# Two weight rows of the last column slab moved from the casting queue to five DMA engines of the hardware queue, cast on chip

## The chip, the cores and the metric

The kernel runs on one core of one Trainium2 chip. The metric is the device time of one execution in microseconds, as the median of several; the profile gives the span of one execution, about 1.8 us less. Before the change the time is 177.0 to 177.1 us.

## The reference, cut to what matters

Attention over 64 heads of 576 tokens (plain and dilated windows) gives `x`, 4608 tokens by 512. A soft mixture of experts follows; only its end matters here.

```python
logits = x @ phi                       # 32 slots, 4 per expert
slot_input = softmax_over_tokens(logits).T @ x
for e in range(8):
    h = np.maximum(slot_input[e] @ w1[e], 0.0)
    slot_out[e] = h @ w2[e]            # w2[e]: 1024 x 512, float32
out = softmax_over_slots(logits) @ slot_out    # 4608 x 512, float32
```

All eight `w1` and `w2` come from HBM as float32 and are used as bf16. The output is 9.44 MB of float32.

Of the kernel before, what the change touches and what calls it, by code (L numbers as in the profile page):

```python
# [7 lines left out]
ACTF = mybir.ActivationFunctionType  # L8
# [6 lines left out]
DM = H * D  # L15
# [43 lines left out]
class Sched:  # L59
# [8 lines left out]
    def op(self, eng, fn, dur, prio, reads=(), writes=(), rmw=(), after=(), banks=(), name="",  # L68
           kind="c", nbytes=0, rate=422e3, lag=0.0, sem=None, tail=False):
        o = Op()  # L70
        o.eng, o.fn, o.dur, o.prio, o.name = eng, fn, dur, prio, name
        o.kind, o.bytes, o.rate, o.lag, o.sem, o.tail = kind, nbytes, rate, lag, sem, tail
        o.deps, o.succ = set(), []
        o.banks, o.opens, o.ord = [], [], None
        o.seq = len(self.ops)
        for a in after:
            if a is not None:
                o.deps.add(a)
        for b in reads:
            o.deps.update(b.w)  # L80
            b.r.append(o)
        for b in writes:
            if b.r:
                b.prev = b.w + b.r
                b.w, b.r = [], []
            o.deps.update(b.prev)
            b.w.append(o)
        for b in rmw:
            o.deps.update(b.prev)
            o.deps.update(b.w)  # L90
            o.deps.update(b.r)
            b.w.append(o)
        for b in list(reads) + list(writes) + list(rmw) + list(banks):
            if isinstance(b, Bank) and b not in o.banks:
                o.banks.append(b)
                if b.left == 0:
                    o.opens.append(b)
                b.left += 1
        o.deps.discard(o)
        self.ops.append(o)  # L100
        return o
# [99 lines left out]
def bass_dilated_sliding_attn__then__soft_moe_slots_kernel(  # L201
# [15 lines left out]
    def take(n):  # L217
        o = top[0]
        top[0] = o + (n + 1) // 2 * 2
        return o  # L220
# [4 lines left out]
    o_kqv = [o_w2 + 3 * 8 * DM, take(3 * 2304)]  # L225
# [36 lines left out]
    def a(off, dims, p0=0, pn=128):  # L262
        return AP(ar, p0 * NBF + off, [[NBF, pn]] + dims)
# [4 lines left out]
    def af(off, dims, p0=0, pn=128):  # L268
        return AP(ar_f.tensor, (p0 * NBF + off) // 2, [[NBF // 2, pn]] + dims)
# [4 lines left out]
    def pf(bank, off, dims, p0=0, pn=128):  # L274
        return AP(ps, p0 * 4096 + bank * 512 + off, [[4096, pn]] + dims)
# [6 lines left out]
    op = sc.op  # L282
    PE, ACT, DVE, POOL, SP = "PE", "ACT", "DVE", "POOL", "SP"
    pe, act, dve, pool, spq = nc.tensor, nc.scalar, nc.vector, nc.gpsimd, nc.sync
# [4 lines left out]
    def actt(n, extra=0.0):  # L289
        return 0.2 + extra + n / 1200.0  # L290

    def dvet(n, psum=False):
        return ((120 if psum else 58) + n) / 960.0
# [3 lines left out]
    b_stg = [[[Buf(f"stg{i}{j}{x}") for x in range(2)] for j in range(3)] for i in range(NSTG)]  # L297
    b_kqv = [[[Buf(f"kqv{i}{j}{x}") for x in range(2)] for j in range(3)] for i in range(2)]
# [15 lines left out]
    b_w2h = [[Buf(f"w2h{x}{s}") for s in range(2)] for x in range(4)]  # L314
# [3 lines left out]
    def w2off(e):  # L318
        return o_w2 + e * 8 * DM if e < 5 else o_stg + (e - 5) * 8 * DM


    def sem(n):
        return [nc.alloc_semaphore(n), 0]

    s_stg = [[[sem(f"s_in{i}{j}{x}") for x in range(2)] for j in range(3)] for i in range(NSTG)]
    loads = {}
# [23 lines left out]
    wq = []  # L350
# [28 lines left out]
    def w2_slab(e, s, c0=0, n=8):  # L379
        def fn():  # L380
            return pool.dma_start(  # L381
                a(w2off(e) + 256 * s + c0 * DM, [[DM, n], [1, 256]]),
                moe_w2[e].rearrange("(p c) f -> p c f", c=8)[:, c0:c0 + n, 256 * s:256 * s + 256])
        return (fn, n << 17, f"w2s_{e}{s}{c0}", [b_w2[e][s] if e == 6 else b_w2h[(0, 4, 6, 7).index(c0)][s]])
# [1 line left out]
    wq += [w1_piece(e, 2 if e == 0 else 0) for e in range(8)]  # L386
    wq += [w2_piece(e) for e in range(6)] + [w2_piece(6, 0, 4)]
    for s in range(2):
        wq += [w2_slab(6, s, 4, 4), w2_slab(7, s, 0, 4), w2_slab(7, s, 4, 2),
               w2_slab(7, s, 6, 1), w2_slab(7, s, 7, 1)]  # L390
    nw = [0]

    def load_w(n):
# [17 lines left out]
       kind="dma", nbytes=1 << 20, sem=sem("s_w1f"), writes=b_w2[0], name="w1f")  # L411
# [401 lines left out]
    for x, y in zip(dma_order, dma_order[1:]):  # L813
# [4 lines left out]
    T1 = NH * PERIOD + 12.0  # L818
    op(DVE, lambda: dve.tensor_reduce(f(o_rcol, [[1, 1]]), f(o_csp, [[1, 16]]),
                                      mybir.AxisListType.X, AluOp.add), .2, T1, reads=[b_csp],  # L820
       writes=[b_rcol], name="cs")
# [4 lines left out]
    def sd_fn(bank=bank):  # L826
# [10 lines left out]
       reads=[bank], writes=[b_sit], name="sid")  # L837
    row_sums(5, 1, T1 + 4)
    for x in range(2):
# [12 lines left out]
        for g in range(2):  # L852
            op(PE, lambda g=g, l1_fn=l1_fn: l1_fn(g), pet(4, 760), T1 + 0.2 + x + .5 * g,
               reads=[b_sit] + b_w1[4 * g:4 * g + 4], rmw=[bank], name=f"L1{g}{x}")
# [3 lines left out]
            writes=[b_hsb[x], b_p[0], b_p[1]], name=f"RL{x}")  # L858
# [10 lines left out]
    for g in range(2):  # L869
# [3 lines left out]
           reads=[bank], writes=[b_htz], name=f"HE{g}")  # L873
# [5 lines left out]
    def l2(es, x, col, n, cs=range(8), bufs=None):  # L879
# [22 lines left out]
       name="SOx")  # L902
    op(DVE, lambda: dve.tensor_copy(af(o_sx, [[1, 512]], 64, 64), pf(sobank[0].idx, 0, [[1, 512]], 64, 64)),
       dvet(512, True), T1 + 10, reads=[sobank[0]], writes=[b_sx, b_p[2]], name="SOy")
    for x in (1, 2):
        l2((6,), x, 256 * x - 256, 256, range(4, 8), [b_w2[6][x - 1]])
        for y, cs in enumerate((range(4), range(4, 6), range(6, 7), range(7, 8))):
            l2((7,), x, 256 * x - 256, 256, cs, [b_w2h[y][x - 1]])
        op(DVE, lambda x=x: dve.tensor_tensor(  # L909
            a(o_so + 256 * x - 256, [[1, 256]], 64, 64), pf(sobank[x].idx, 0, [[1, 256]], 64, 64),  # L910
            af(o_sx + 512 * x - 512, [[1, 256]], 64, 64), AluOp.add), dvet(256, True),
           T1 + 10 + 20 * x, reads=[sobank[x], b_sx], writes=[b_so[x - 1]], name=f"SO{x - 1}")



    NA = 2.5
    b_og = [[[Buf(f"og{G}{j}{s}") for s in range(2)] for j in range(n)] for G, (_, n) in enumerate(GROUPS)]
    store_ops = []
    ne = [0]
# [2 lines left out]
    def ostg(G):  # L922
        return o_w1 + 8 * GROUPS[G][0]
# [6 lines left out]
    def out_tile(G, j, c0, cw, prio):  # L930
        bank = Bank(f"o{G}{j}{c0}")
        t0, n = GROUPS[G]
        rd = [b_so[s] for s in range(2) if c0 < 256 * (s + 1) and c0 + cw > 256 * s]
        op(PE, lambda: pe.matmul(pf(bank.idx, 0, [[1, cw]]), a(o_et + t0 + j, [[n, 128]]),  # L934
                                 a(o_so + c0, [[1, cw]]), start=True, stop=True),
           pet(1, cw), prio, reads=[b_et] + rd, writes=[bank], name=f"O{G}{j}{c0}")
        dst = af(ostg(G) + 2 * (512 * j + c0), [[1, cw]])
        src = lambda: pf(bank.idx, 0, [[1, cw]])
        wr = [b_og[G][j][s] for s in range(2) if c0 < 256 * (s + 1) and c0 + cw > 256 * s] + over(G)
        sca = f(rcol(G) + j, [[1, 1]])  # L940
        if ne[0] % 2 == 0:
            op(ACT, lambda: act.activation(dst, src(), ACTF.Copy, scale=sca), actt(cw, .1),  # L942
               prio + .1, reads=[bank, b_rinv], writes=wr, name=f"OE{G}{j}{c0}")
        else:
            op(DVE, lambda: dve.tensor_scalar(dst, src(), sca, None, op0=AluOp.mult),  # L945
               dvet(cw, True) + .08, prio + .1, reads=[bank, b_rinv], writes=wr, name=f"OE{G}{j}{c0}")
        ne[0] += 1

    def store(G, c0, cw, prio, j0, n):
        t0, nj = GROUPS[G]  # L950
        rd = [b_og[G][j][s] for j in range(j0, j0 + n) for s in range(2)
              if c0 < 256 * (s + 1) and c0 + cw > 256 * s]
        dst = out[t0:t0 + 128 * nj, c0:c0 + cw].rearrange("(p j) f -> p j f", j=nj)[:, j0:j0 + n, :]
        src = af(ostg(G) + 2 * (512 * j0 + c0), [[512, n], [1, cw]])
        store_ops.append(op(SP, lambda: spq.dma_start(dst, src), .1, prio, kind="dma",
                            nbytes=128 * n * cw * 4, rate=347e3 if cw < 512 else 420e3,
                            sem=sem(f"s_o{G}{c0}{j0}"), reads=rd, name=f"ST{G}{c0}{j0}"))

    T2 = T1 + 40
    halves = [(n // 2, n % 2 * 2) for n in range(int(2 * NA))]  # L960
    for G, x in halves:
        for j in (x, x + 1):
            out_tile(G, j, 0, 256, T1 + 20 + G + .25 * x)
        store(G, 0, 256, T1 + 20 + G + .25 * x + .2, x, 2)
    for G, x in halves:
        for j in (x, x + 1):
            out_tile(G, j, 256, 256, T2 + 10 + G + .25 * x)
        store(G, 256, 256, T2 + 10 + G + .25 * x + .2, x, 2)
    for G, js in [(2, (2, 3))] + [(G, range(8)) for G in range(3, 6)]:
        for j in js:  # L970
            out_tile(G, j, 0, 512, T2 + 10 + G + .1 * j)
            if j == js[-1] or G == 3 and j == 3:
                n = 4 if G == 3 else len(js)
                store(G, 0, 512, T2 + 10 + G + .1 * j + .05, j + 1 - n, n)
# [11 lines left out]
    for o in order:  # L986
        c = o.sem if o.kind == "dma" else ctr[o.eng]
# [4 lines left out]
        for d in o.deps:  # L992
            if d.eng == o.eng == PE:
                continue
            s, val = d.ev
# [60 lines left out]
```

## The kernel before: the parts that the change touches

GpSimd issues nearly all loads on the software queue, which casts on the way. The last 1.5 experts of `w2` come as two column slabs of 256 columns each (`s`), in ever smaller pieces, so that the first half of the output columns can be computed and stored while the second slab still loads.

```python
def w2_slab(e, s, c0=0, n=8):
    def fn():
        return pool.dma_start(
            a(w2off(e) + 256 * s + c0 * DM, [[DM, n], [1, 256]]),
            moe_w2[e].rearrange("(p c) f -> p c f", c=8)[:, c0:c0 + n, 256 * s:256 * s + 256])
    ...
for s in range(2):
    wq += [w2_slab(6, s, 4, 4), w2_slab(7, s, 0, 4), w2_slab(7, s, 4, 2),
           w2_slab(7, s, 6, 1), w2_slab(7, s, 7, 1)]
...
for x in (1, 2):                       # x = 1, 2: first and second column half
    l2((6,), x, 256 * x - 256, 256, range(4, 8), ...)
    for y, cs in enumerate((range(4), range(4, 6), range(6, 7), range(7, 8))):
        l2((7,), x, 256 * x - 256, 256, cs, [b_w2h[y][x - 1]])
    op(DVE, ... dve.tensor_tensor(..., AluOp.add) ...)   # L909: "the add" of each half
```

After each add come the output tiles of 128 tokens: one matmul, one scaling copy out of PSUM (ScalarE and VectorE in turn), and stores on SyncE's hardware queue. Ten tiles (2.5 groups of four) are made by halves: their left columns after the first add, their right ones after the second. The other 26 are made whole, after the second add. "Cover" below means the stores of left halves, which keep the DMA engines busy until the second add lets the others go.

The softmax here doesn't subtract the row's maximum and nothing guards it: scores larger than these inputs give would overflow.

## Time and profile before

| | before |
|---|---|
| time, median | 177.03 us (176.88 to 177.2) |
| span of the profiled execution | 175.2 us |
| last weight row landed | 151.54 us |
| second add (L909) begins | 151.90 us |
| first store of the second half issued, landed | 153.35, 155.31 to 155.66 us |
| last store landed | 174.75 us |

Three more lines of the page say how the tail is fed. The first two are the scaling copies of the output tiles (busy time, mean ns, idle before); the third is the half-tile stores (KB each, us from issue to landing).

```profile
L942 ACT ACTIVATE ar<-ps,fs 128x512 f32<-128x512 f32 (+1 forms) x23 | 11.4, 636 | 5.7 <-PE ps L934 5.7
L945 DVE TENSOR_SCALAR ar<-ps,fs 128x512 f32<-128x512 f32 (+1 forms) x23 | 12.7, 627 | 1.0 <-PE ps L934 1.0
out_dram<-ar SPq DMA_DIRECT2D x10, 256.0 KB, 3.1
```

The mean of 0.63 us mixes half and whole tiles; a whole one takes about 0.75 us on either engine. So the two make a 262 KB tile every 0.38 us, faster than the queue drains it at about 430 GB/s (0.61 us). So once the second add is done the tail is stores alone, and its end is set by when they can begin and how many bytes are left then.

### The profile page before, as it was taken

To read this page: it belongs to the slowest core of one execution; us is meant where nothing else is said; L and a number is where in the kernel's file an instruction comes from. 1 tells how busy PE (TensorE), PEld (TensorE's weight loads), DVE (VectorE), ACT (ScalarE), POOL (GpSimd) and SP (SyncE) were. 2 spreads that over 40 slices of the span, in tenths; PEclk is the share of its full clock that TensorE was granted. 3 is DMA by queue.
4 is the path that set the end of the run, shared out by engine and by line. 5 is a ranking of instruction groups with operands and counts; after the bars stand their busy time and mean duration, and the time that the engine had idled before them with its cause. 6 is when DMAs were issued, how large, how long until landed. Compare 5 with 4: busy or idle time off the path is not lost.

```text
span 175.2 us, 4785 instructions
## 1 busy us (share of the span) xinstructions
PE 127.4 (73%) x2102; PEld 86.0 (49%) x2102; DVE 120.7 (69%) x220; ACT 105.1 (60%) x165; POOL 44.5 (25%) x90
## 2 busy tenths in 40 slices
PE   0008667969998998998988997999776766898000
PEld 0005535746766866776756766776343323442000
DVE  6899497978998998998698798349430002699300
ACT  2404763797978969969868968965603001599000
POOL 7659502406234053027200014940000000000000
PEclk9999995699999999999999999999999999999655
DMA  6999999999999999999999999999999999999997
GB/s 191 228 210 217 211 214 208 219 210 213 216 211 214 217 213 207 218 211 217 213 209 216 217 213 221 215 219 211 209 223 215 210 192 189 270 343 418 449 423 299
DMA packets 14388, 41.26 MB, mean 236 GB/s; under 512 B 1696, under 2 KB 7328, under 8 KB 12064
## 3 DMA queue, kind: packets, MB, share of 16 engines
q0 software_dynamic: 10512, 30.41, 88.3%
q1 hardware_dynamic: 3856, 10.55, 15.7%
q8 instruction: 16, 0.26, 0.5%
q14 instruction: 4, 0.03, 0.0%
HBM read 61.93 MB, written 9.44 MB: 407 GB/s over the span
## 4 chain that ended last, share of the span: by engine, by line
DMA 33%; DVE 24%; PE 22%; ACT 7%; POOL 5%; issue 3%; POOLq 0%; DVEq 0%
DMA ar<-in_moe_w_dram 21%; DMA ar<-in_v_dram 12%; PE ps L529 6%; DVE ar L497 6%; DVE ar L945 6%; ACT ar L568 4%; POOL ar L381 3%; DVE ar L503 3%; PE ps L590 2%; PE ps L713 2%; PE ps L536 2%; DVE ar L634 2%; PE ps L623 2%; PE ps L546 2%; DVE ar L454 2%
## 5 line engine op out<-in xcount | busy, mean ns | idle before, releaser
L568 ACT ACTIVATE ar<-ps 128x1152 bf16<-128x1152 f32 (+1 forms) x32 | 37.9, 1186 | 21.5 <-PE ps L553 10.9
L529 PE MATMUL ps<-ar 128*128 128x320 bf16 (+1 forms) x128 | 23.2, 306 | 16.1 <-DVE ar L503 13.8
L497 DVE STREAM_TRANSPOSE ar<-ar 128x576 uint32<-128x576 uint32 x28 | 32.8, 1237 | 0.6 <-DMA ar<-in_v_dram 0.6
L634 DVE TENSOR_TENSOR ar<-ps,fs 96x768 bf16<-96x768 f32 (+1 forms) x32 | 26.3, 822 | 1.1
L596 ACT ACTIVATE ar<-ps 128x768 bf16<-128x768 bf16 x32 | 24.8, 809 | 3.6 <-PE ps L590 3.1
L529 PEld LDWEIGHTS ps<-ar 128*128 128x128 bf16 x128 | 10.8, 100 | 20.9 <-POOL ar L427 13.7
L623 PE MATMUL ps<-ar 128*128 128x65 bf16 x320 | 15.2, 195 | 3.4 <-ACT ar L568 2.1
L590 PE MATMUL ps<-ar 128*128 128x128 bf16 x192 | 15.8, 229 | 2.4 <-DVE ar L634 2.1
L503 DVE STREAM_TRANSPOSE ar<-ar 128x576 uint32<-128x576 uint32 x12 | 14.6, 1241 | 1.8 <-DMA ar<-in_q_dram 1.8
L623 PEld LDWEIGHTS ps<-ar 128*128 128x128 bf16 x320 | 12.1, 98 | 6.7 <-ACT ar L568 2.9
L345 POOL DMA_DIRECT2D ar<-in_k_dram x14 | 7.5, 541 | 30.5 <-DVE ar L497 15.6
L942 ACT ACTIVATE ar<-ps,fs 128x512 f32<-128x512 f32 (+1 forms) x23 | 11.4, 636 | 5.7 <-PE ps L934 5.7
L590 PEld LDWEIGHTS ps<-ar 128*128 128x128 bf16 x192 | 12.7, 118 | 3.7 <-DVE ar L634 2.3
L630 DVE RECIPROCAL fs<-ps 96x12 f32<-96x12 f32 (+1 forms) x32 | 6.5, 203 | 10.9 <-PE ps L623 10.6
L885 PE MATMUL ps<-ar 128*32 128x512 bf16 (+1 forms) x76 | 10.8, 347 | 4.3 <-DMA ar<-in_moe_w_dram 3.3
L945 DVE TENSOR_SCALAR ar<-ps,fs 128x512 f32<-128x512 f32 (+1 forms) x23 | 12.7, 627 | 1.0 <-PE ps L934 1.0
L934 PE MATMUL ps<-ar 128*128 128x512 bf16 (+1 forms) x46 | 10.2, 346 | 1.1 <-DVE ar L909 1.0
L343 POOL DMA_DIRECT2D ar<-in_q_dram x16 | 8.8, 549 | 6.1 <-DVE ar L509 6.1
L713 PE MATMUL ps<-ar 128*128 128x288 bf16 x64 | 9.8, 299 | 0.7 <-ACT ar L697 0.7
L693 ACT ACTIVATE ar<-ps 128x1024 bf16<-128x1024 bf16 x8 | 8.2, 1030 | 3.3 <-PE ps L680 3.3
L690 ACT ACTIVATE ar<-ps 128x576 bf16<-128x576 bf16 x16 | 9.5, 648 | 1.1 <-PE ps L674 0.8
L509 DVE STREAM_TRANSPOSE ar<-ar 128x160 uint32<-128x160 uint32 (+1 forms) x32 | 9.6, 413 | 0.0
(78 smaller groups left out, 190.2 us busy)
## 6 DMA issues: line engine op xcount, KB each, us to landing
ar<-in_moe_w_dram POOLq DMA_DIRECT2D x13, 1024.0 KB, 26.6
ar<-in_k_dram POOLq DMA_DIRECT2D x16, 288.0 KB, 14.5
ar<-in_q_dram POOLq DMA_DIRECT2D x16, 288.0 KB, 16.2
ar<-in_v_dram POOLq DMA_DIRECT2D x16, 288.0 KB, 15.2
out_dram<-ar SPq DMA_DIRECT2D x2, 2048.0 KB, 10.1
out_dram<-ar SPq DMA_DIRECT2D x10, 256.0 KB, 3.1
out_dram<-ar SPq DMA_DIRECT2D x2, 1024.0 KB, 6.1
ar<-in_moe_w_dram SPq DMA_DIRECT2D x1, 1024.0 KB, 4.9
```

What stands on the lines that cost most here:

```text
L497: return dve.transpose(au(o_kqv[kq] + 2304 * j + 36 * x, [[1, 18], [36, 16], [576, 2]]), au(src + 64 * 18 * x, [[32, 18], [1, 32]]))
L503: return dve.transpose(au(dst, [[1, 18], [18, 32]]), au(src, [[32, 18], [1, 32]]))
L529: pe.matmul(pf(h, 0, [[1, W]]), a(o_id, [[1, 128]]), a(msk, [[1, W]]), start=True, stop=False)
L568: eo = op(ACT, lambda P=P, W=W: act.activation(a(P, [[W, 4], [1, W]]), AP(ps, 0, [[4096, 128], [512, 4], [1, W]]), ACTF.Exp, scale=SCALE), ...
L590: last = pe.transpose(pb(bank.idx, bb * 256 + par * 32, [[64, 4], [1, 32]]), src, a(o_id, [[1, 128]]))
L596: op(ACT, lambda t=t, bank=bank: act.activation(a(o_vb[vs] + 3 * t * VBK, [[66, 12], [2, 32], [1, 2]]), pb(bank.idx, 0, [[64, 12], [1, 32] ...
L623: last = pe.matmul(pf(bank.idx + x, 65 * t, [[1, 65]]), w, a(VB + t * VBK + 66 * h, [[1, 65]]), start=True, stop=True)
L634: op(DVE, lambda hp=hp, bank=bank: dve.tensor_tensor(a(ox + 128 * hp, [[64, 2], [256, NT], [1, 64]], 0, rows), pf(bank.idx, 0, [[512, 2], ...
L713: last = pe.matmul(pf(bank.idx, 0, [[1, 288]]), a(o_phis + 128 * c, [[1, 128]]), a(o_xt[xt] + 576 * c + 288 * g, [[1, 288]]), start=(c == ...
L885: last = pe.matmul(pf(sobank[x].idx, 0, [[1, n]], 32 * j, 32), a(o_htz + 1024 * g + 128 * c + 32 * j, [[1, 32]]), a(w2off(e) + DM * c + co ...
L942: op(ACT, lambda: act.activation(dst, src(), ACTF.Copy, scale=sca), actt(cw, .1), prio + .1, reads=[bank, b_rinv], writes=wr, name=f"OE{G} ...
L945: op(DVE, lambda: dve.tensor_scalar(dst, src(), sca, None, op0=AluOp.mult), dvet(cw, True) + .08, prio + .1, reads=[bank, b_rinv], writes= ...
```

## The change

The last two rows of the second slab leave the casting queue. They come as float32 on the hardware queue into a buffer that attention has finished with, gated by the landing of the first slab's last row. The transfer is cut as 125 + 3 partitions. ScalarE casts one row, VectorE the other. The intent is visible in the shape: some DMA engines run ahead of others at the end, so let a few carry the last rows while the casting queue ends earlier on all. As it should then end earlier, one tile fewer is made by halves.

```diff
-        wq += [w2_slab(6, s, 4, 4), w2_slab(7, s, 0, 4), w2_slab(7, s, 4, 2),
-               w2_slab(7, s, 6, 1), w2_slab(7, s, 7, 1)]
+        wq += [w2_slab(6, s, 4, 4), w2_slab(7, s, 0, 4), w2_slab(7, s, 4, 2)]
+        wq += [w2_slab(7, s, 6, 1), w2_slab(7, s, 7, 1)] if s == 0 else []
...
+    for p0, pn in ((0, 125), (125, 3)):
+        op(SP, lambda p0=p0, pn=pn: spq.dma_start(
+            af(o_kqv[1], [[1, 512]], p0, pn),
+            moe_w2[7].rearrange("(p c) f -> p c f", c=8)[p0:p0 + pn, 6:8, 256:512]), .1, T1 + 8,
+           kind="dma", nbytes=pn * 2048, sem=sem(f"s_w7t{p0}"), after=[loads["w2s_707"]], ...)
+    for c in (0, 1):
+        dst, src = a(w2off(7) + (6 + c) * DM + 256, [[1, 256]]), af(o_kqv[1] + 512 * c, [[1, 256]])
+        ...  # c = 1: dve.tensor_copy(dst, src); c = 0: act.activation(dst, src, ACTF.Copy)
...
-    NA = 2.5
-    halves = [(n // 2, n % 2 * 2) for n in range(int(2 * NA))]
+    halves = [(0, 0, 2), (0, 2, 2), (1, 0, 2), (1, 2, 2), (2, 0, 1)]
...
-    for G, js in [(2, (2, 3))] + [(G, range(8)) for G in range(3, 6)]:
+    for G, js in [(2, (1, 2, 3))] + [(G, range(8)) for G in range(3, 6)]:
```

## The prediction

> **What bounds the kernel now.** I read the page first: no compute engine is above 73% of the span, while the row of DMA shares reads 9 in nearly every slice and 71.4 MB cross between HBM and the core in 175.2 us. So the kernel is a stream of transfers with computing beside it. Then I read the end of the chain of waits, because a stream that never pauses can only gain where it is late or uneven.
>
> ```profile
> DMA  6999999999999999999999999999999999999997
> GB/s 191 228 210 217 211 214 208 219 210 213 216 211 214 217 213 207 218 211 217 213 209 216 217 213 221 215 219 211 209 223 215 210 192 189 270 343 418 449 423 299
> q0 software_dynamic: 10512, 30.41, 88.3%
> q1 hardware_dynamic: 3856, 10.55, 15.7%
> q8 instruction: 16, 0.26, 0.5%
> HBM read 61.93 MB, written 9.44 MB: 407 GB/s over the span
> ```
>
> The GB/s row counts bytes as written, so the casting loads (32 bits in, 16 out) show about 210 and the stores about 430. The loads end in the slice that shows 270. From there to the end it is stores. The pieces of the chain in 140 to 176 us (start, length, what) say what joins the two:
>
> ```profile
> 115.33 36.21 DMA ar<-in_moe_w_dram
> 151.54 0.04 issue
> 151.58 0.30 PE ps L885
> 151.88 0.02 issue
> 151.90 0.44 DVE ar L909
> 152.34 0.05 issue
> 152.39 0.42 PE ps L934 x2
> ```
>
> The last weight row lands at 151.54, one matmul and the add L909 make the second half of the slot outputs by 152.34, and only then can the second half's output tiles be made. The first store of that half is issued at 153.35 and lands at 155.31 to 155.66. Busy time by stretch (columns: length; PE, PEld, DVE, ACT, POOL; clock, DMA share, GB/s) shows whether DMA pauses meanwhile:
>
> ```profile
> 147.50:148.50 1.00, 0.48 (x3) 0.29 (x4) 0.43 (x1) 0.00 (x0) 0.00 (x0) 1.00 1.44 193
> 148.50:150.00 1.50, 1.47 (x14) 1.13 (x12) 1.26 (x4) 1.37 (x4) 0.00 (x0) 1.00 0.86 115
> 150.00:151.50 1.50, 1.41 (x9) 0.51 (x7) 0.79 (x3) 0.56 (x2) 0.00 (x0) 1.00 1.12 279
> 153.00:154.00 1.00, 1.00 (x9) 0.66 (x7) 1.00 (x3) 1.00 (x4) 0.00 (x0) 1.00 1.03 361
> 154.00:154.50 0.50, 0.50 (x4) 0.27 (x2) 0.50 (x3) 0.50 (x2) 0.00 (x0) 1.00 0.79 275
> ```
>
> At 148.5 the rate falls from 193 to 115, to 60%, with loads still queued: a part of the DMA engines has finished its share. The trace's semaphore records agree. Each transfer counts sixteen steps, one per DMA engine, and the steps of the very last row fall in two groups: seven at 148.69 to 149.21, one at 149.77, eight at 151.05 to 151.54. **Half of the engines run about 2.3 us late.** The first stores fill the early half from 150.16. The five first-half stores then land every 0.76 us, in the early engines until 154.29, in the late ones until 154.98. So the late engines have no gap before the store that lands at 155.5, and the early ones one of about 0.25 us (the 0.79). There is very little left to gain.
>
> **What the Trainium skill says.** "DMA: Bandwidth & Descriptors", section "Why a DMA increments its semaphore by 16 and not by 1": a hardware-queue transfer uses the largest number of engines up to 16 that divides the slowest dimension, and these are "the lowest-numbered k of the core's 16". 125 partitions give 5, and 3 give 3. The old kernel has no such transfer, so the trace can't confirm it. The same page, "Queues, rings and completion order": an engine with work on two queues takes packets from them in turn. The trace agrees as far as it goes: between 150 and 151.5 loads and stores advance together. "Runtime: NRT & Kernel Launch", "Instruction fetch mechanics": instructions are refilled in 16 KiB blocks by DMA. The trace has 16 such packets of 0.26 MB together, about 0.95 us each; six had passed by 64 us and just then six of sixteen engines were about 1 us late, and after sixteen it is eight that are about 2.3 us late. So the lateness looks like two refills on each of eight engines. **No page says which eight.** "VectorE: DVE Perf Modes", the section on the TRN2 errata: a copy between SBUF tiles costs 224 cycles plus one per element at 1.2 GHz on ScalarE, and 58 plus the elements over the mode's factor at 0.96 GHz on VectorE. For 1024 elements ScalarE gives 1.04 us, and the trace has 1.048 us for the 128x1024 cast at L413, so I trust it for 256 elements.
>
> **The change part by part.**
> *Removed:* the last two rows of the second column slab, each 131 KB in HBM, from the software queue. They are the last two of its transfers, landing at 151.15 and 151.54 after 150.80. The casting queue ends 0.74 us sooner, on every engine, early and late.
> *Added, transfer:* the same 262 KB as 32-bit data by five engines. The gate is the landing of the first slab's last row at 147.44. Add 0.06 to react; 1.0 from issue to first packet (0.91 at the first store, 1.00 at the early load of w1); then 25 partitions x 2 rows = 50 packets of 1 KB per engine. The only 1 KB packets on this queue are stores at 46 ns, so 2.3 us, and 0.05 for the three further partitions; and 0.35 from the last packet to the landing, as the first store shows. Sum: 147.44 + 0.06 + 1.0 + 2.35 + 0.35 = **151.2**, if these five engines are early ones, whose software work ends near 148. That is 0.34 sooner than 151.54.
> *Added, casts:* row 6 on ScalarE 480 cycles = 0.40, row 7 on VectorE 186 cycles = 0.19 (estimates from the skill's formula), side by side. Both engines have finished the first-half tiles at 150.6. With 0.1 for semaphores the matmul of row 6 starts 0.5 after the landing, instead of 0.04, and that of row 7 about 0.1 behind it. Landing to add was 0.36 and becomes about 0.96.
> *The add* starts at 151.2 + 0.96 = 152.15 instead of 151.90: **0.25 later**. This is the step that sets the end.
> *Moved:* one tile leaves the halves. The first half writes nine half tiles instead of ten, so 0.13 MB (0.38 us at 0.76 per pair) goes behind the second add; in the second half nine instead of ten save 0.38, and the later full-width store grows from two tiles (1.27 us) to three (1.9). Sum behind the add: -0.38 + 0.63 = +0.25 us.
> *The end:* the first second-half store begins at 154.25 in the early engines now, and at 154.64 in the late ones, which decide. After the change everything waits for the add: 154.25 + 0.25 = 154.5 in all engines. The late half gains 0.14, and the 0.25 of extra volume is lost: +0.1 us. Span 175.3, time **177.1** by this sum. I state 177.0, as an author who chose a count as odd as five probably knew which engines are early.
>
> **The rivals.**
> (1) *The five engines are among the late ones.* Then the load meets about 2 us of casting work there: 148.5 + 2.0 + 2.3 + 0.35 = 153.1, the add begins near 154.1, 2.1 late, and the time is about 179. For it: nothing tells the numbers of the late eight. Against it: the shape 125 + 3 makes sense only if low engines have room. I give it a quarter.
> (2) *The late engines are the bound and the relief counts in full.* If packets from HBM are shorter than 46 ns, or the landing quicker, the add comes at 151.7, the late engines are 0.7 ahead, and only the volume moves: 176.5. For it: the late engines have no gap now. Against it: 1 KB store packets never ran faster than 44 ns.
> (3) *The transfer is hidden anyway.* Stores fill the queues until 154.0, so an add a little later costs nothing. With a tile less in front there is less to hide behind: 4.5 pairs from 150.75 end at 154.1 in the five engines, the others before, so the cover ends 0.4 before 154.5. I expect a small new gap instead.
>
> **Range and chances.** With early engines (three quarters) I expect 176.4 to 177.7, the add's time being uncertain by 0.5 us; with late ones 178.3 to 179.5. Eight in ten lie between 176.4 and 178.6. Faster by over 2% would mean under 173.5, which the volume of the stores alone rules out: 1%. Slower by over 2% means past 180.6, worse than rival (1): 2%.
>
> **What would show it.** The hardware load should be issued near 147.5 and land near 151.2; landing at 153 shows rival (1). The last software piece should land near 150.8. The casts should take 0.40 and 0.19 us, and L927, the second add, begin near 152.15. DMA shares under 0.9 about 154 would be the new gap; none there, with an add at 151.7, would be rival (2). The prediction is wrong if the packets of the new load take much more than 46 ns, if more or fewer than five engines carry it, or if the first add (147.81) moves.

## More of the kernel before

A small scheduler in the program orders the instructions of each engine by estimated times.

## The result, and the profile after

The changed kernel takes 178.5 us in the median (178.21 to 178.59, six runs), the kernel before 177.12 beside it. The ratio is 1.0074 (1.006 to 1.0088): slower by three quarters of a per cent, clear of noise, and the same within 2%. Here and below a ratio is the mean time of one kernel's runs over that of the other's runs of the same rounds, so it is not quite the ratio of the medians.

The profiled execution was the fastest of the six (178.21 us, span 176.4). Its page has almost the same transfers:

```profile
GB/s 189 232 210 214 212 212 212 218 209 213 219 209 214 221 208 212 222 206 214 219 207 214 217 216 215 215 217 212 219 214 217 202 195 184 301 281 417 451 427 297
q0 software_dynamic: 10224, 30.28, 87.1%
q1 hardware_dynamic: 3864, 10.81, 15.9%
HBM read 61.93 MB, written 9.44 MB: 405 GB/s over the span
```

From before to after, 0.13 MB left the casting queue (as bf16) and 0.26 MB came to the hardware queue (as float32). The slice that showed 343 GB/s now shows 281: the loss lies between 154 and 158 us. The chain of waits in 140 to 177 us (start, length, what) shows how the second add is reached:

```profile
147.55 0.04 issue
147.60 0.30 PE ps L885
147.89 0.07 SPq L909
147.96 0.05 issue
148.01 3.89 DMA ar<-in_moe_w_dram
151.90 0.02 issue
151.92 0.02 ACTq L1023
151.94 0.05 issue
151.99 0.42 ACT ar L921
152.41 0.04 issue
152.46 0.41 PE ps L885 x2
152.86 0.02 issue
152.89 0.44 DVE ar L927
```

Line numbers moved: L909 is now the new load, L921 the ScalarE cast, L927 the add. The load is the last thing to land, at 151.90, where the casting queue's last row had landed at 151.54. A cast and a second matmul then stand between landing and add: 0.99 us, where it was 0.36. The add is 0.99 later than before. Busy time by stretch (length; PE, PEld, DVE, ACT, POOL; clock, DMA share, GB/s) shows what the stores did meanwhile:

```profile
153.00:154.00 1.00, 0.63 (x6) 0.63 (x7) 0.60 (x2) 0.18 (x1) 0.00 (x0) 1.00 0.92 323
154.00:154.50 0.50, 0.50 (x6) 0.39 (x4) 0.50 (x2) 0.50 (x2) 0.00 (x0) 1.00 0.17 57
154.50:155.00 0.50, 0.50 (x4) 0.19 (x2) 0.50 (x3) 0.50 (x3) 0.00 (x0) 1.00 0.01 2
155.00:155.50 0.50, 0.50 (x4) 0.30 (x3) 0.50 (x2) 0.50 (x3) 0.00 (x0) 1.00 0.45 154
```

From 154.0 to 155.5 the shares 0.17, 0.01 and 0.45 leave 0.5 x (0.83 + 0.99 + 0.55) = 1.2 us in which the DMA engines have nothing to do. Before there was 0.1 (the 0.79). This gap is the loss, by a theory that e1 and e3 test below. The first store after it lands at 156.33 to 156.53, last step 0.87 later than before, and from there to the end it is 19.43 us where it was 19.09, for the tile moved behind the add. 0.87 + 0.34 = 1.21, and the last store lands at 175.96, 1.21 after the old 174.75.

The semaphore records of the trace tell how the DMA engines fared. Each transfer posts sixteen steps; on the hardware queue those of the unused engines are posted at once. These are the steps of the last software piece, and of the two parts of the new load:

```
last software piece   148.19 148.25 148.34 148.41 148.45 148.50 148.71 | 149.25 | 150.21 150.28 150.49 150.53 150.57 150.58 150.69 150.90
125 partitions        (148.09)  151.19 151.26 151.71 151.73 151.86
3 partitions          (148.58)  151.37 151.49 151.90
```

As before, seven engines are early, one is in the middle, eight are late. The new load ran on five engines, and none delivers as a late engine with this load would, near 153.

### The profile page after: what moved, and what is told of

The parts are those of the page before. It is cut to its first block, busy times and chain, and to the rows that moved or that the text cites. A ratio compares the mean times of both kernels' runs of the same rounds, so it can differ in the third digit from the quotient of the medians.

```text
span 176.4 us, 4785 instructions
## 1 busy us (share of the span) xinstructions
PE 128.1 (73%) x2101; PEld 86.2 (49%) x2101; DVE 120.5 (68%) x220; ACT 105.7 (60%) x166; POOL 43.5 (25%) x88
## 4 chain that ended last, share of the span: by engine, by line
DMA 34%; DVE 24%; PE 22%; ACT 5%; POOL 3%; issue 3%; DVEq 0%; SPq 0%; ACTq 0%
DMA ar<-in_moe_w_dram 22%; DMA ar<-in_v_dram 12%; PE ps L529 6%; DVE ar L497 6%; DVE ar L962 6%; PE ps L590 3%; ACT ar L568 3%; DVE ar L503 2%; DVE ar L634 2%; PE ps L536 2%; PE ps L713 2%; PE ps L623 2%; PE ps L546 2%; DVE ar L454 2%; POOL ar L381 2%
## 5 line engine op out<-in xcount | busy, mean ns | idle before, releaser
L529 PEld LDWEIGHTS ps<-ar 128*128 128x128 bf16 x128 | 10.8, 101 | 21.0 <-POOL ar L427 13.7
L590 PE MATMUL ps<-ar 128*128 128x128 bf16 x192 | 16.4, 234 | 2.3 <-DVE ar L634 2.0
L623 PEld LDWEIGHTS ps<-ar 128*128 128x128 bf16 x320 | 12.2, 98 | 6.7 <-ACT ar L568 2.8
L885 PE MATMUL ps<-ar 128*32 128x512 bf16 (+1 forms) x76 | 11.9, 376 | 4.3 <-DMA ar<-in_moe_w_dram 2.4
L590 PEld LDWEIGHTS ps<-ar 128*128 128x128 bf16 x192 | 13.1, 120 | 3.7 <-DVE ar L634 2.3
L885 PEld LDWEIGHTS ps<-ar 128*32 128x32 bf16 x76 | 4.8, 101 | 11.1 <-DMA ar<-in_moe_w_dram 5.4
L713 PE MATMUL ps<-ar 128*128 128x288 bf16 x64 | 9.2, 287 | 0.9 <-DVE ar L791 0.6
```

Of the source, the lines that this page charges most:

```text
L529: pe.matmul(pf(h, 0, [[1, W]]), a(o_id, [[1, 128]]), a(msk, [[1, W]]), start=True, stop=False)
L590: last = pe.transpose(pb(bank.idx, bb * 256 + par * 32, [[64, 4], [1, 32]]), src, a(o_id, [[1, 128]]))
L623: last = pe.matmul(pf(bank.idx + x, 65 * t, [[1, 65]]), w, a(VB + t * VBK + 66 * h, [[1, 65]]), start=True, stop=True)
L713: last = pe.matmul(pf(bank.idx, 0, [[1, 288]]), a(o_phis + 128 * c, [[1, 128]]), a(o_xt[xt] + 576 * c + 288 * g, [[1, 288]]), start=(c == ...
L885: last = pe.matmul(pf(sobank[x].idx, 0, [[1, n]], 32 * j, 32), a(o_htz + 1024 * g + 128 * c + 32 * j, [[1, 32]]), a(w2off(e) + DM * c + co ...
```

## The experiments

**Theory A**: the loss is a gap in the stores, because the second add is late; the add is late by two terms, a load that lands later instead of sooner and casts that stand on the path behind it. Rivals: the bytes on the hardware queue take time from the stores (B); the regrouping of the tiles costs it (C); the casts alone (D) or the hardware queue alone (I); the five engines have no room (E).

| run | second add | time, us | ratio to before (95%) |
|---|---|---|---|
| before | 151.90 | 177.0 to 177.1 | 1 |
| changed kernel | 152.89 | 178.50 | 1.0074 (1.006 to 1.0088) |
| e1, changed, 10 half tiles | 153.01 | 178.21 | 1.0062 (1.005 to 1.0074) |
| e3, changed, 12 half tiles | 153.41 | 177.74 | 1.0042 (1.003 to 1.0054) |
| e2, before, 9 half tiles | 151.84 | 177.18 | 1.0011 (0.9999 to 1.0023) |
| e7, before, 12 half tiles | 152.13 | 177.15 | 1.0008 (0.9996 to 1.0021) |
| e12, rows uncast on the software queue | 152.64 | 177.83 | 1.0043 (1.0029 to 1.0056) |
| e5, load issued early | 153.24 | 178.36 | 1.0066 (1.0052 to 1.0079) |
| e4, load on 15 engines | 152.55 | 177.97 | 1.0053 (1.0041 to 1.0065) |
| e6, load on 16 engines | 152.40 | 177.83 | 1.0042 (1.003 to 1.0054) |
| e8, 15 engines, issued early | 153.08 | 178.13 | 1.0059 (1.0041 to 1.0076) |
| e9, the same, 10 half tiles | 153.04 | 178.26 | 1.0074 (1.0057 to 1.0092) |
| e10, one row only | 151.71 | 177.00 | 0.9999 (0.9987 to 1.0012) |
| e11, one row, 10 half tiles | 151.75 | 176.95 | 0.9997 (0.9983 to 1.001) |

The add is that of the profiled execution of each (for e5 its slowest, 178.77), the time the median of five or six. The experiments ran on three chips, each time with the kernel before beside them, whose medians there were 177.00 to 177.07.

### Is it the gap? e1, e3, e2, e7

The number of half tiles alone was changed, in either kernel. In e1:

```diff
-    halves = [(0, 0, 2), (0, 2, 2), (1, 0, 2), (1, 2, 2), (2, 0, 1)]
+    halves = [(0, 0, 2), (0, 2, 2), (1, 0, 2), (1, 2, 2), (2, 0, 2)]
-    for G, js in [(2, (1, 2, 3))] + [(G, range(8)) for G in range(3, 6)]:
+    for G, js in [(2, (2, 3))] + [(G, range(8)) for G in range(3, 6)]:
```

e3 and e7 add `(2, 2, 2)` to that and leave group 2 out of the whole tiles; e2 is the kernel before with the nine half tiles of the change.

> The changed kernel with the old ten half tiles per half (five pairs) instead of nine. Theory A (the add begins about 1 us later, and the stores run dry meanwhile, so each tile written in front of the add saves its own time): the second add stays near 152.9, the gap in the stores shrinks from about 1.2 to about 0.85 us, and the time is about 178.15 us, 0.35 under the changed kernel's 178.5. Rival B (the loss comes from the load taking DMA time from the stores, no gap involved): tiles in front or behind make no difference, 178.5.

> The changed kernel with twelve half tiles per half. Theory A: three more half tiles in front of the add are 1.15 us of stores at 0.38 us each, so the gap closes though the add stays at 152.9; with about 0.1 to 0.2 for more 1 KB rows, 177.4 to 177.6 us. Rival B (DMA time, not a gap): 178.5 or a little more.

> The kernel before with nine half tiles per half, the other half of the change alone. Theory A: the add stays at 151.9 and the cover in front of it shortens by 0.35 us, which the late engines nearly have to spare; 177.1 to 177.4 us. Rival C (the regrouping itself costs what the change lost): about 178.4.

> The kernel before with twelve half tiles per half. Theory A (its late engines have no gap before the second add's stores, its early ones 0.25 us): more cover buys nothing there, and two more tiles in 1 KB rows cost 0.1 to 0.2: 177.0 to 177.3 us, where the same step gave 0.8 us in the changed kernel. Rival B: no difference between the two kernels in what cover gives.

In the changed kernel cover pays: from 178.50 to 178.21 with one half tile more and to 177.74 with three. By the intervals of the ratios only the step to three is clear; that of e1 overlaps the changed kernel's. The add did not come sooner in these runs; it came later, by 0.1 and 0.5, so e3 missed its 177.4 to 177.6. The stretches of e1 show the gap shrunk but not gone:

```profile
154.00:154.50 0.50, 0.50 (x7) 0.43 (x5) 0.50 (x2) 0.50 (x2) 0.00 (x0) 1.00 0.96 338
154.50:155.00 0.50, 0.50 (x5) 0.32 (x3) 0.50 (x2) 0.50 (x3) 0.00 (x0) 1.00 0.19 64
155.00:155.50 0.50, 0.50 (x4) 0.29 (x2) 0.50 (x2) 0.50 (x3) 0.00 (x0) 1.00 0.27 92
```

The idle time is 0.5 x (0.04 + 0.81 + 0.73) = 0.8 us, 0.4 less than in the changed kernel. In e3 it is 0.4 (shares of 0.67 and 0.53 from 155 to 156). In the kernel before, nine, ten and twelve half tiles take 177.18, 177.0 and 177.15: cover buys nothing where there is no gap. So B and C fall. The regrouping costs a gap's worth only where a gap stands; alone it is within the noise. The idle share is an average over the engines, not a price to the tenth: e2 has 0.3 us of it (0.82 in 153 to 154, 0.71 in 154 to 154.5) and its median is only 0.15 us above the kernel before, with an interval that includes no loss.

### What makes the add late? e12

The same two rows, still uncast and still cast by ScalarE and VectorE, were loaded by the software queue on all sixteen engines. The instructions of the compute engines and their order are those of the changed kernel.

```diff
-    for p0, pn in ((0, 125), (125, 3)):
-        op(SP, lambda p0=p0, pn=pn: spq.dma_start(...), ..., after=[loads["w2s_707"]], ...)
+    wq += [(lambda: pool.dma_start(
+        af(o_kqv[1], [[1, 512]]),
+        moe_w2[7].rearrange("(p c) f -> p c f", c=8)[:, 6:8, 256:512]), 2 << 17, "w2s_7uncast", ...)]
```

> The changed kernel with the same two rows, still uncast and still cast by ScalarE and VectorE, but loaded by the software queue on all sixteen engines as its last transfer; every compute engine has the same instructions in the same order. This leaves the casts on the path and takes the hardware queue away. Theory A (the loss is the sum of about 0.6 us of casts between landing and add and 0.4 us of a later landing): the rows land near 151.6 as in the kernel before, the second add begins 0.93 to 1.0 us after that, near 152.5, and the time is 177.9 to 178.1 us, between the two kernels. Rival D (the casts alone make the loss): the landing in the changed kernel is no later than here, and the time is 178.4. Rival I (the hardware queue alone makes the loss): 177.1.

Its chain, with other line numbers for the same things (L919 the ScalarE cast, L925 the add):

```profile
151.72 0.02 issue
151.74 0.43 ACT ar L919
152.16 0.04 issue
152.21 0.41 PE ps L890 x2
152.61 0.02 issue
152.64 0.44 DVE ar L925
```

The rows land at 151.72, about when they did in the kernel before, and the add comes 0.92 later instead of 0.36. The time is 177.83, between the two kernels, if a little under the range expected: 0.76 over the 177.07 measured beside it. With casts on the path and without the hardware queue half of the loss is there, so neither D nor I holds alone. The rest goes with the later landing. The profiled executions understate it: they landed 0.18 apart, while the medians differ by 0.67, and the profiled execution of the changed kernel was its fastest.

### Why does the load land late? e5, e4, e6, e10

**Issued earlier (e5).** The load was gated by a piece that lands near 143.5 (`lag` is for the scheduler only, and keeps the order of instructions as it was).

```diff
-           kind="dma", nbytes=pn * 2048, sem=sem(f"s_w7t{p0}"), after=[loads["w2s_707"]],
+           kind="dma", nbytes=pn * 2048, lag=1.0, sem=sem(f"s_w7t{p0}"), after=[loads["w2_60"]],
```

> The changed kernel with the new load issued when the third-last full-width weight piece has landed (about 143.5) instead of the first slab's last row (147.5); the instructions of every engine keep their order. Theory A (the load is late because it is issued late; five engines early by 2.3 us have the room for it): it lands near 149.5, the casts are done before the last software piece lands at 150.9, the second add begins near 151.4, the first add does not move, and the time is 176.9 to 177.3 us. Rival D (the casts and the longer way from landing to add cost it): 178.2 or more. Rival E (the five engines have no room): the first add moves from 147.9 to about 149, and the time does not improve.

From e5's instructions in order of time:

```profile
143.57 0.78 SPq L909 DMA_DIRECT2D ar<-in_moe_w_dram  x2
147.91 0.43 DVE L927 TENSOR_TENSOR ar<-ps,ar 64x256 bf16<-64x256 f32 x1 [2.61 <-PE ps L885]
152.34 0.42 ACT L921 ACTIVATE ar<-ar 128x256 bf16<-128x256 f32 x1 [1.62 <-DMA ar<-in_moe_w_dram]
153.24 0.43 DVE L927 TENSOR_TENSOR ar<-ps,ar 64x256 bf16<-64x256 f32 x1 [0.60 <-PE ps L885]
```

This expectation failed. Issued 4 us sooner, the load landed at 152.32, no sooner than before. The packet records say why: its first packet moved at 147.22, 3.65 us after the issue, against about 0.9 in the changed kernel. With the software queue full on those engines, the hardware queue's packets did not take turns from the start; they waited. Once they moved they came 95 ns apart on an engine, where in the changed kernel they came 42 apart. Four of the five engines then delivered at 150.87 to 151.21, and the fifth at 152.32. The software piece of rows 4 and 5, too, was completed at 152.14 by one engine instead of at 150.90. The fifth is, by its steps, the one in the middle: in this execution it was 0.95 us behind the early ones (142.16 against 141.03 to 141.23 on an earlier piece). It delivered 1.3 us after the mean of the other four, of which its own lag would account for 0.95; the rest is open. Rival E holds for this engine; the first add did not move. This profile also had a granted clock of 0.50 from 154 to 156, where the changed kernel has 1.00, and its first store was issued 1.68 us after the add instead of 1.48.

**Fewer packets per engine (e4, e6).**

```diff
-    for p0, pn in ((0, 125), (125, 3)):
+    for p0, pn in ((0, 120), (120, 8)):      # e4
+    for p0, pn in ((0, 128),):               # e6
```

> The changed kernel with the same load cut 120 + 8 partitions[...]; everything else as it was. Theory F (four of the five engines are early, one is a middle engine that finishes its software share 0.4 to 0.9 us after them, and its 50 packets end last; engines 5 to 7 are early too): the packets take 1.4 us, the load lands between 150.4 and 151.1 instead of 151.9, the second add begins near 151.8 instead of 152.9, and the time is 177.3 to 177.7 us. Rival G (engines 5 to 7 are among the late eight): their steps come after 151.9, and the time is 178.6 or more.

> The changed kernel with one load of 128 partitions on all sixteen engines, 16 packets each. Theory F: the early engines deliver by 149.8, the late ones begin only when their software share is done near 150.55 and deliver by 151.6 to 151.8; the second add begins near 152.6 and the time is 178.1 to 178.4 us, little better than the changed kernel, because the late engines carry the bytes again. Rival H (the number of packets per engine alone decides the landing): it lands near 150, and the time is about 177.2.

e4 was misplanned. I wanted eight engines with 30 packets each, but by the rule that the prediction cites the largest divisor of 120 up to 16 is 15, and the trace shows fifteen steps. Both runs put bytes back on the late engines, and both loads fall into two groups: in e6 eight steps at 149.67 to 149.91 and eight at 150.86 to 151.48. Packets on early engines do land early (2.4 us after the issue with 16 packets each), but the landing of the whole is that of the late engines. It came at 151.48 in e6 and 151.63 in e4, still sooner than on five engines, and the add followed 0.92 later in both. So e6 did better than expected, 177.83 for 178.1 to 178.4. The 8-partition rest of e4 is on engines 0 to 7 by the Trainium skill ("DMA: Bandwidth & Descriptors", "Why a DMA increments its semaphore by 16 and not by 1"; the trace has eight steps but doesn't number them). It delivered its steps at 149.64 to 150.14 on six and at 151.45 and 151.54 on two: so, if the rule holds, of the eight lowest engines only six had room in this run.

**Issued early on fifteen engines (e8, e9)** was planned with the same wrong count.

> As the one on eight engines, but the load is issued when the last full 2 MB piece has landed, at about 141.3; the instructions of the compute engines keep their order. A load issued to busy engines began 3.65 us after its issue in the early-gate run, so its packets begin near 145 and take turns with the software packets. Theory F: it lands before 149.5, the casts are done before the last software piece at 150.9, the software piece is not delayed, the second add begins at 151.4 to 151.6, the first add stays at 147.9, and the time is 176.8 to 177.2 us. Rival E (no room): the last software piece lands after 151.3 or the first add moves, and the time is 177.5 or more.

> The same with ten half tiles per half, as before the change. Theory A: with the add near 151.5 the stores in front of it last until about 154, so one more half tile in front saves up to 0.3 us: 176.5 to 177.0 us, at or a little under the kernel before (177.0). Rival: the stores are no longer short of work, and it is equal to the run with nine.

The edits are those of e4 with the gate at `w2_50`, and for e9 also e1's. The load landed by 147.3, yet it delayed the late engines' share of the first slab: its last row landed at 148.60 in e8 instead of 147.55, the first add at 149.19 instead of 147.92, and the last software piece at 151.95. Both have a higher median than e6, though e8's interval overlaps that of e6. Two more things stood in their way: the granted clock was 0.56 and 0.50 from 150 to 151.5 us, where the other profiles have 1.00, and in e8 the cast on ScalarE came behind the output tiles of the first half and ended at 152.6. So they show that early bytes on late engines delay the first add, and decide nothing about eight engines. Their first packets moved 3.6 us after the issue, as in e5.

**One row instead of two (e10, e11).** Row 6 stays with the casting queue, row 7 goes to the five engines in 25 packets each and is cast by VectorE.

```diff
-        wq += [w2_slab(7, s, 6, 1), w2_slab(7, s, 7, 1)] if s == 0 else []
+        wq += [w2_slab(7, s, 6, 1)] + ([w2_slab(7, s, 7, 1)] if s == 0 else [])
-            moe_w2[7].rearrange("(p c) f -> p c f", c=8)[p0:p0 + pn, 6:8, 256:512]), ...
+            moe_w2[7].rearrange("(p c) f -> p c f", c=8)[p0:p0 + pn, 7, 256:512]), ...
-    for c in (0, 1):
+    for c in (1,):
```

> The changed kernel with only the last row on the hardware queue (25 packets per engine on the same five engines instead of 50, cast by VectorE); row 6 stays with the software queue. Theory A (load late, then casts on the path): issue near 147.6, first packet 0.9 later, 1.15 us of packets plus the 0.3 to 0.5 us of long packets that every five-engine load showed, 0.35 to land: 150.4 to 150.9, so that the cast is done before the last software piece lands near 151.2. The second add begins at 151.6 to 151.7, sooner than in the kernel before (151.9), and the time is 176.7 to 177.0 us. Rival D (any load through the hardware queue plus cast costs more than it saves): the add comes after 151.9 and the time is 177.4 or more.

> The same with ten half tiles per half. Theory A: the late engines have no gap and the early ones a small one, so the tenth tile gives 0 to 0.3 us: 176.6 to 176.9 us, under the kernel before. Rival: equal to the run with nine or worse.

The 125-partition part landed at 150.57 in e10 and 150.58 in e11, and the cast was done by 151.15, before the last software row at 151.24 and 151.28. The add came at 151.71 and 151.75, as expected, and the loss is gone: 177.00 and 176.95. But the expected gain did not come; both equal the kernel before. In e10 the stores run short between 153 and 154.5:

```profile
153.00:154.00 1.00, 1.00 (x8) 0.54 (x6) 1.00 (x4) 1.00 (x4) 0.00 (x0) 1.00 0.79 277
154.00:154.50 0.50, 0.50 (x4) 0.33 (x3) 0.50 (x2) 0.50 (x2) 0.00 (x0) 1.00 0.89 289
```

In e11, with one half tile more, they do not:

```profile
153.00:154.00 1.00, 1.00 (x8) 0.64 (x6) 1.00 (x4) 1.00 (x4) 0.00 (x0) 1.00 1.04 351
154.00:154.50 0.50, 0.50 (x4) 0.24 (x3) 0.50 (x2) 0.50 (x3) 0.00 (x0) 1.00 1.02 340
```

With no gap left the bytes alone set the end: e11's first store of the second half lands at 155.25 to 155.47, 0.1 to 0.2 us sooner than in the kernel before, and that is all that this version had to gain. A tie is the best that this idea gave in these runs; no version beat both kernels clearly.

The two sizes also measure the load by itself. From the issue to the landing of the 125-partition part, 25 packets per engine took 3.01 and 2.95 us (e10, e11), and 50 took 4.23, 4.30 and 4.32 (the changed kernel, e1, e3). So 25 packets more cost 4.28 - 2.98 = 1.30 us, 52 ns each with whatever pauses fell among them; drawn on to no packets, an estimate, this leaves 1.7 us that go with the transfer whatever its size.

## Why the prediction was right or wrong, point by point

It said no change beyond 2% and gave 176.4 to 178.6 us; 178.50 lies just inside. That is luck: for early engines, which is what the trace shows, it gave 176.4 to 177.7, and 178.50 is 0.8 outside. Only the chance it left for late engines, which did not hold, stretched the range so far. The point, 177.0, was 1.5 us too low.

- **The bound** was read rightly: stores without a pause, almost nothing to gain. e2 and e7 show that the kernel before is not short of cover.
- **Five engines, early ones:** five steps, as predicted. The rule that the prediction cites for the number of engines held wherever it was tried: 125 partitions gave 5 steps, 120 gave 15, 8 gave 8, 3 gave 3, and 128 gave 16. Rival (1), five late engines, fell: the steps came by 151.9. But one of the five was, by its times, the middle engine, and the load waited for it. The packet records show four chains of 1 KB packets beginning at 148.52 to 148.60 and a fifth at 148.93, just ahead of the middle engine's software step at 149.25.
- **The casting queue ends sooner**, near 150.8: measured 150.90.
- **The step that failed: "151.2, if these five engines are early ones".** It landed at 151.86, and the rest at 151.90, so the sum for the transfer was mis-sized by 0.7 us. About 0.1 of it is a gate that opened at 147.55 instead of 147.44. The rest is in the transfer: 4.28 us from issue to landing on average over three runs, where 1.0 + 2.35 + 0.35 = 3.7 was predicted. Two engines did land at 151.19 and 151.26, at the predicted moment. The other three were 0.5 to 0.65 late: one is the middle engine, with one packet of 320 ns on it, and the packet records, which can be followed by their ends, suggest that two others paused for 0.4 to 0.5 us halfway. Other runs have single packets of up to 531 ns, in place of 46. The cost per packet, 46 ns taken from the stores, was not what failed: of the 163 packets of the load recorded up to 150.35, 140 took 46 ns, and in an unbroken row they start 42 apart. The slope of 52 has pauses in it. Why single packets and engines stall so is open. That the sum for a transfer needs every engine to be on time, and the wait is for the last, is what the working left out.
- **The casts:** landing to add 0.96 predicted, 0.99 measured; ScalarE 0.42 for 0.40. VectorE took 0.29 for 0.19, beside it and hidden.
- **The volume behind the add:** 0.25 predicted, 0.34 measured. The single half tile's store took about 0.55 us, not half of a pair's 0.76.
- **The end:** "a small new gap" of 0.4 us was stated in rival (3), and it was 1.2. (Its 150.75 for the start of the cover in the five engines isn't derived; its own 151.2 - 0.35 gives 150.85 and a gap of 0.2. Its 150.6 for the end of the first-half tiles holds for ScalarE; VectorE ended at 150.8. Neither matters to the sum.) The add was 0.74 later than the predicted 152.15, and nearly all of that went into the gap. The predicted 177.1 plus 0.74 and the 0.09 of volume is 177.9. The profiled execution took 178.21, and the median of the six is 0.3 above it, so 0.6 us between this sum and the median are not placed; one profile cannot show what differs between executions.
- **Rival (2)**, relief in full for the late engines, needed an add at 151.7. e10 and e11 have that and gave 177.0, not the 176.5 stated for it. They relieve the late engines of one row and not of two, so this is not a full test of it.
- That the lateness of eight engines comes from instruction refills stays argued. Eight late engines and one or two in between stood in every run with the old gate, but no run took the refills away.

## What to carry to other kernels

Moving bytes from a full queue to another one helps only if the transfer, counted from when its gate opens to the last of its engines, ends before the queue it leaves would have, and its after-work (here a cast, 0.6 us) ends too. Where stores fill a wait, ask how long they last: a delay costs nothing as long as they do and its whole length afterwards, so don't cut the cover in the change that makes the wait uncertain. And size such a transfer for the slowest engine in its set: half the rows on the hardware queue (e10) removed the whole loss here.

## What the Trainium skill lacked or had wrong

- "DMA: Bandwidth & Descriptors", "Queues, rings and completion order", says that an engine takes turns between the queues it has work for, packet by packet. A hardware-queue load issued to engines full of software packets moved its first packet 3.65 us after the issue (e5), and the small phi load of the kernel before 3.7 us after it (issued 11.85, first packet 15.54), against 0.9 to 1.0 on engines without such work. In e8 and e9 it was 3.6. The page has no figure for this wait.
- The same page, "Latency and other measured facts", names engines 7 and 15 as usually slower. Here eight of sixteen are late: in the kernel before seven had posted their last step by 149.21, one at 149.77 and eight from 151.05 to 151.54. The page has no late half, nor which one it would be.
- The same page gives a bandwidth per engine, but no time for a load of 1 KB rows on few engines, nor for pauses in it: here a packet took 46 ns as a rule, and single ones up to 531; between 25 and 50 packets per engine the landing moved by 52 ns per packet, with 1.7 us besides.
- "VectorE: DVE Perf Modes", the section on the TRN2 errata: its table (58 cycles and half an element each) gives 0.19 us for the cast of 256 float32 elements to bf16; it took 0.294. The fixed term of about 150 cycles that the same section calls measured gives (150 + 128) / 0.96 GHz = 0.29 us, an estimate that fits. Its ScalarE row gives 0.40, measured 0.416.
